# Batch 0 of a chunked attention with a sine network: values computed transposed, normalisers spread by TensorE, memory values loaded apart, and a new order of the opening

## The chip, the cores and the metric

The kernel runs on one core of a Trainium2 chip. The metric is the device time of one execution in microseconds (us); a kernel's time is the median of its runs. The engines are written as in the profile: PE (TensorE matmuls), PEld (its weight loads), DVE (VectorE), ACT (ScalarE), POOL (GpSimd), SP (SyncE). Each engine works through its own list of instructions in order and waits where data from another engine or from a DMA is not there yet.

## The reference

Two parts follow each other. First a chunked attention over 4 batches, 8 heads, 768 positions of 64 numbers each, in 24 chunks of 32 queries. A chunk sees 8 memory keys, and the positions from 16 ahead of it to 8 behind it:

```python
k_full = np.concatenate([mem_k, k_ctx], axis=2)
v_full = np.concatenate([mem_v, v_ctx], axis=2)
scores = scale * np.matmul(q_c, k_full.transpose(0, 1, 3, 2))
scores = scores - np.max(scores, axis=-1, keepdims=True)
a = np.exp(scores)
a = a / (np.sum(a, axis=-1, keepdims=True) + 1e-09)
out[:, :, c_start:c_end] = np.matmul(a, v_full)
```

Then a network with a sine in it, on the 3072 positions with their 8 heads side by side (512 numbers):

```python
h = x @ w_in                      # 512 x 2048
s = np.sin(alpha * h)
g = h + s * s / (alpha + 1e-09)
return (g @ w_out).astype(np.float32)   # 2048 x 512
```

Inputs and output are fp32; the kernel multiplies in bf16.

## The kernel before

**Stages.** Everything is unrolled. A batch is 768 positions, cut into 8 windows of 96 queries (QW, three chunks each), a half is 4 windows (HALF, 384 queries). The opening ("front", stage -1) does the attention of batch 0. Then stage i (0 to 3) does the network of batch i, with the attention of batch i + 1 woven in. In a stage, `half_tile` (L422) makes one half of a tile of 128 of the 2048 inner columns with 4 matmuls against w_in (L424), `sine`, `squared` and `finish` (L435 to L456) make g of it, and `second` (L458) multiplies with w_out (L462).

**Order.** The order is written out by hand: a string of words per stage, read by `Stage.run` (L525); the first letter picks the method, the rest are its arguments. This order is the order of the instructions on each engine; there is no other scheduler. The words of the front:

- `a` n engine: cast tile n of the fp32 loads (0 to 3 are k of head pairs 0 to 3, 4 to 7 q) to bf16, L653
- `k`, `l`: turn a head pair's k or q on PE (12 transposes, L274); `K`, `L`: copy it out of PSUM into kT or qT (L285, L291, L299)
- `s` hp half: masked scores of a head pair and a half on PE (L317, L325), then the exponential on ACT into a tile pt (L332)
- `v` hp half: values (L344), then normalising on DVE (L353, L354) into x_blk; `t`, `T`: turn x_blk on PE (L366) and copy it into xT on DVE or ACT (L369). xT is what the network of stage 0 reads
- `V` b h0 h1: load v of heads h0 to h1 with POOL's DMAs (L172, L179; L168 too for head 0); the windows overlap, so rows come twice, and the DMA casts to bf16
- `dm`: load all memory values with one POOL DMA (L665); `m` 0: spread those of batch 0 into rows 64 to 71 of vw on DVE (L188)
- `C` x: constants: `b`, `m`, `i` for the mask, `k` the memory keys (cast L767, turned L771, copied L775 and into kT L207), `l` alpha (turned L785, L786, L787), `p`, `z`, `v`, `s` memsets on POOL
- `I` a b: load columns of w_in by tiles on POOL's queue (L213); `U`: rows of w_out (L219)
- `z` n: n matmuls of zeros (L686); `We`, `Ws`: one small Exp or Sin on ACT (L699), by which the table of that function is loaded
- stage 0 goes on with `o8 b0 h0 ...`: `b` and `h` are the two halves of a tile of the network

**Queues.** SP's queue brings the eight fp32 loads of k and q of batch 0 (L708, 384 KB each), ACT's the memory keys (L716, twice) and alpha (L717), POOL's all that is cast on its way: v, the weights, later k and q. `Banks` (L59) hands out the 8 PSUM banks; a bank given back may be taken again at once, and the new user then waits on the chip for the old one's last reader. It prefers a bank whose neighbour is in use.

**Values before.** In `u_values` (L339) the exponentials are the stationary operand and V, with a column of ones, moves, so that the queries lie on the partitions of the result and its column 64 holds the sums:

```python
nc.tensor.matmul(
    otv[:, e, i, :], pt[:, HALF * e + QW * i:HALF * e + QW * i + P],
    vws[b % 2][:, 2 * hp + e, 4 * half + i, 0:D + 1],
)
```

`normed` (L350) divides by it and `u_turn` (L372) turns the block, because the network needs the 512 numbers on partitions.

## Time and profile before

| what | value |
|---|---|
| time, median of 3 runs | 215.51 us (215.49 to 216.0) |
| span of the profiled execution (first to last instruction) | 213.1 us |
| instructions | 4479 |
| busy: PE, PEld, DVE, ACT, POOL | 201.7, 113.5, 140.5, 143.5, 99.8 us |
| granted clock of TensorE | 1.000 |
| DMA | 28.19 MB, mean 132 GB/s |

The profiled execution has no time of its own beside its span; the 2.4 us between the span and the median lie around the instructions. All starts below are us from the first instruction. In a timeline row stand start, duration, engine, line, operation, what is written and read, the shape, how many instructions are merged into the row, and in brackets how long the engine was idle ahead of it and what released it. "DMA" rows of the chain run from a transfer's issue to its landing. A row of a DMA issue ends with the KB of one transfer and the median us from issue to landing.

### The profile page before, as it was taken

What the parts mean: (1) busy time and instruction counts of PE and PEld (TensorE: products, weight loads), DVE (VectorE), ACT (ScalarE), POOL (GpSimd) and SP (SyncE); (2) the same over time, 40 slices, a digit from 0 to 9 for tenths busy, and PEclk for the clock granted to TensorE, in tenths of its full rate; (3) what the DMA queues carried; (4) which work ended last, traced back from release to release, by engine and by line L of the source; (5) the groups of instructions that cost most, each with busy time, mean ns of one, the idle gap of its engine ahead of it and who ended that gap; (6) DMA issues with size and microseconds to landing.
All of it is one profiled execution on the core that took longest, in us unless ns stands there. A gap on an engine that the chain in (4) does not pass through costs nothing.

```text
span 213.1 us, 4479 instructions
## 1 busy us (share of the span) xinstructions
PE 201.7 (95%) x1721; PEld 113.5 (53%) x1721; DVE 140.5 (66%) x218; ACT 143.5 (67%) x230; POOL 99.8 (47%) x140
## 2 busy tenths in 40 slices
PE   0799899999999999999999999999999999999994
PEld 0456555565455556555455555554555555554443
DVE  7598678999542749975856649898157197865011
ACT  2597898976857469977846199887846289891110
POOL 8959515688598193009991039659400023200000
PEclk9999999999999999999999999999999999999999
DMA  6999999999999999969999229989945400000312
GB/s 195 337 163 141 193 209 205 204 163 182 131 177 141 137 148 144 180 88 110 126 217 171 72 63 131 156 126 129 175 115 123 124 15 0 2 3 0 148 49 98
DMA packets 95908, 28.19 MB, mean 132 GB/s; under 512 B 84864, under 2 KB 92432, under 8 KB 95888
## 3 DMA queue, kind: packets, MB, share of 16 engines
q0 software_dynamic: 68736, 13.25, 92.3%
q1 hardware_dynamic: 26976, 14.62, 28.2%
q8 instruction: 13, 0.21, 0.4%
q14 instruction: 7, 0.06, 0.1%
q10 hardware_dynamic: 176, 0.04, 0.1%
HBM read 29.66 MB, written 6.29 MB: 169 GB/s over the span
## 4 chain that ended last, share of the span: by engine, by line
PE 71%; DVE 9%; DMA 7%; ACT 4%; issue 4%; POOL 3%; DVEq 0%; POOLq 0%; ACTq 0%
PE ps L462 38%; PE ps L424 27%; DMA memv_st<-in_mem_v_dram 4%; DVE gT L451 4%; DVE s L447 3%; DMA vw<-in_v_dram 3%; PE ps L414 3%; PE ps L385 2%; ACT u L439 2%; PE ps L366 1%; ACT s L444 1%; POOL s L447 1%; POOL vw L172 1%; DVE kT L285 1%; ACT L699 1%
## 5 line engine op out<-in xcount | busy, mean ns | idle before, releaser
L462 PE MATMUL ps<-w_out_sb,gT 128*128 128x512 bf16 (+2 forms) x400 | 89.1, 371 | 0.0
L424 PE MATMUL ps<-xT,w_in_sb 128*128 128x384 bf16 x512 | 86.0, 326 | 0.7 <-DVE gT L451 0.4
L451 DVE SCALAR_TENSOR_TENSOR gT<-s,inv_alpha,ps 128x768 bf16<-128x768 f32 x64 | 63.0, 1011 | 12.5 <-ACT s L444 5.2
L424 PEld LDWEIGHTS <-w_in_sb 128*128 128x128 bf16 x512 | 49.8, 98 | 35.4 <-issue 2.1
L439 ACT ACTIVATE u<-ps,alpha_sb 128x768 f32<-128x768 f32 x64 | 56.6, 895 | 16.8 <-PE ps L424 14.3
L462 PEld LDWEIGHTS <-gT 128*128 128x128 bf16 x400 | 36.6, 98 | 37.9 <-DVE gT L451 0.2
L447 POOL TENSOR_TENSOR s<-u 128x768 f32<-128x768 f32 x11 | 17.4, 1582 | 69.7 <-ACT u L439 69.7
L399 ACT ACTIVATE pt<-ps,biasm 128x256 bf16<-128x256 f32 x72 | 27.2, 489 | 10.5 <-PE ps L385 10.5
L469 DVE COPY o_sb<-ps 128x512 f32<-128x512 f32 (+1 forms) x15 | 10.1, 678 | 28.3 <-PE ps L462 26.4
L447 DVE TENSOR_TENSOR s<-u 128x768 f32<-128x768 f32 x23 | 21.9, 953 | 7.8 <-ACT u L439 7.8
L444 ACT ACTIVATE s<-u 128x768 f32<-128x768 f32 x30 | 25.0, 841 | 0.5
L354 DVE TENSOR_TENSOR x_blk<-ps,rinv 96x512 bf16<-96x512 f32 x32 | 22.0, 687 | 1.1
L469 ACT COPY o_sb<-ps 128x512 f32<-128x512 f32 (+1 forms) x10 | 5.6, 562 | 21.6 <-PE ps L462 21.6
L172 POOL DMA_DIRECT2D vw<-in_v_dram x13 | 12.9, 994 | 7.9 <-PE ps L366 5.4
L353 DVE RECIPROCAL rinv<-ps 96x8 f32<-96x8 f32 x32 | 6.4, 200 | 13.5 <-PE ps L414 12.7
L179 POOL DMA_DIRECT2D vw<-in_v_dram x13 | 12.7, 976 | 0.0
L238 POOL DMA_DIRECT2D kst<-in_k_dram x16 | 12.2, 760 | 1.1 <-DMA vw<-in_v_dram 0.8
L232 POOL DMA_DIRECT2D kst<-in_k_dram x16 | 11.3, 708 | 2.3 <-DMA vw<-in_v_dram 1.6
L369 ACT COPY xT<-ps 128x384 bf16<-128x384 bf16 x12 | 5.6, 496 | 8.2 <-PE ps L366 8.2
L245 POOL DMA_DIRECT2D q_bf<-in_q_dram x12 | 10.7, 912 | 0.0
L414 PEld LDWEIGHTS <-pt 128*128 128x128 bf16 x192 | 8.2, 97 | 4.2 <-ACT pt L399 0.3
L414 PE MATMUL ps<-vw,pt 128*128 128x65 bf16 x192 | 8.9, 193 | 0.0
(81 smaller groups left out, 131.4 us busy)
## 6 DMA issues: line engine op xcount, KB each, us to landing
out_dram<-o_sb SPq DMA_DIRECT2D x23, 256.0 KB, 2.3
kq_f<-in_k_dram SPq DMA_DIRECT2D x4, 384.0 KB, 6.5
kq_f<-in_q_dram SPq DMA_DIRECT2D x4, 384.0 KB, 6.0
q_bf<-in_q_dram POOLq DMA_DIRECT2D x12, 128.0 KB, 6.7
w_in_sb<-in_moe_w_in_dram POOLq DMA_DIRECT2D x1, 1152.0 KB, 12.6
vw<-in_v_dram POOLq DMA_DIRECT2D x7, 128.0 KB, 6.7
vw<-in_v_dram POOLq DMA_DIRECT2D x8, 112.0 KB, 7.4
kst<-in_k_dram POOLq DMA_DIRECT2D x14, 64.0 KB, 5.1
```

What stands on the lines that cost most here:

```text
L172: nc.gpsimd.dma_start(vw[0:64, lo:c1, 0:D], win(vflat, a, n, 64))
L179: nc.gpsimd.dma_start(vw[72:128, c0:hi, 0:D], win(vflat, base + QW * c0 + 48, hi - c0, 56))
L354: nc.vector.tensor_tensor(out=x_blk[:].rearrange("p g e d -> p e g d"), in0=otv[0:QW, :, :, 0:D], in1=rinv[:].unsqueeze(3).to_broadcast([Q ...
L399: nc.scalar.activation(pt[:, 0:H * QW].rearrange("p (g e c) -> p g e c", g=2, e=4)[:, :, :, 32 * m:32 * m + 32], sc[:, :, 0:4 * QW].rearra ...
L414: nc.tensor.matmul(otv[:, e, hp, :], pt[:, QW * i:QW * i + P], vws[b % 2][:, 2 * hp + e, j, 0:D + 1],)
L424: nc.tensor.matmul(t["hT"][:, hf, 0:HALF], w_in_sb[:, kt, P * t["ft"]:P * t["ft"] + P], t["xT"][:, kt, HALF * hf:HALF * hf + HALF], start= ...
L439: nc.scalar.activation(t["u"][:], t["hT"][:, :, 0:HALF], ACTF.Sin, scale=alpha_sb[:, ft:ft + 1])
L444: nc.scalar.activation(s2[:], u[:], ACTF.Square)
L447: e.tensor_tensor(out=s2[:], in0=u[:], in1=u[:], op=ALU.mult)
L451: nc.vector.scalar_tensor_tensor(out=gT[:, ft, :].rearrange("p (e c) -> p e c", e=2), in0=t["s2"][:], scalar=inv_alpha[:, ft:ft + 1], in1= ...
L462: nc.tensor.matmul(o[:, c0:c1], gT[:, ft, P * s:P * s + P], w_out_sb[:, ft, c0:c1], start=(ft == 0), stop=(ft == FT - 1),)
L469: copier(state["engines"][state["o"] % len(state["engines"])])(o_sb[:, c0:c1], o[:, c0:c1])
```

## The change

For batch 0 alone:

- the values are computed with V stationary and the exponentials moving, so that the result has the head's 64 numbers on partitions, two heads in the upper and lower half, and goes to xT with one multiplication on DVE; the turning and its copies go away for batch 0
- the sums are made apart (word `n`, for a head pair: 16 matmuls with one column of ones, a reciprocal, and its split into two bf16 parts), and spread over 64 partitions by PE (word `r`: 32 matmuls with a broadcast column as the stationary operand and the identity moving), then copied to SBUF in fp32
- the memory values of batch 0 come in fp32 on ACT's queue and are cast on DVE (`Cw`); `dm` brings the other three batches
- the memory keys are turned in fp32, without the cast ahead of it; `ident_f` is larger, and made in a word of its own (`Cf`)
- the words of the front stand in a new order; those of the stages are the same (their lines are only broken elsewhere)

```diff
+    ones = consts.tile([P, 2], BF, name="ones")
-    memk_bf = memv_st[0:NK, 0]
-    ident_f = consts.tile([FT, FT], F32, name="ident_f")
+    ident_f = consts.tile([4 * FT, 4 * FT], F32, name="ident_f")
...
-    def u_values(b, hp, half, pt):
-        ot, bs = banks.pair()
-        otv = ot[:, :, 0:4 * (D + 1)].rearrange("p e (g c) -> p e g c", c=D + 1)
-        for e in range(2):
+    rs = {}
+
+    def u_sums(hp, two):
+        bank, bs = banks.single()
+        sums = bank[:, 0:2 * H]
+        for half in range(2):
+            for c in range(H):
+                nc.tensor.matmul(sums[:, H * half + c:H * half + c + 1],
+                                 two[half][:, QW * c:QW * c + P], ones[:, 0:1])
+        rinv = blk.tile([QW, 2 * H], F32, name="r_inv", bufs=2)
+        hi = blk.tile([QW, 2 * H], BF, name="r_hi", bufs=2)
+        lo = blk.tile([QW, 2 * H], BF, name="r_lo", bufs=2)
+        nc.vector.reciprocal(rinv[:], sums[0:QW])
+        nc.vector.tensor_copy(hi[:], rinv[:])
+        nc.vector.tensor_tensor(out=lo[:], in0=rinv[:], in1=hi[:], op=ALU.subtract)
+        banks.give(bs)
+        return hi, lo
+
+    def u_spread(hp, got, eng):
+        t, bs = banks.pair()
+        for half in range(2):
             for i in range(4):
+                for part in range(2):
+                    for e in range(2):
+                        c = H * half + 4 * e + i
+                        nc.tensor.matmul(
+                            t[64 * e:64 * e + 64, half, QW * i:QW * i + QW],
+                            got[part][:, c:c + 1].to_broadcast([QW, D]),
+                            ident[0:QW, 0:QW], start=(part == 0), stop=(part == 1),
+                        )
+        rs[hp] = mlp.tile([P, 2, HALF], F32, name="r_sb", tag="s2")
+        copier(eng)(rs[hp][:], t[:, :, 0:HALF])
+        banks.give(bs)
+
+    def u_values(xT, hp, half, pt):
+        bank, bs = banks.single()
+        for i in range(4):
+            for e in range(2):
                 nc.tensor.matmul(
-                    otv[:, e, i, :], pt[:, HALF * e + QW * i:HALF * e + QW * i + P],
-                    vws[b % 2][:, 2 * hp + e, 4 * half + i, 0:D + 1],
+                    bank[64 * e:64 * e + 64, QW * i:QW * i + QW],
+                    vws[0][:, 2 * hp + e, 4 * half + i, 0:D],
+                    pt[:, HALF * e + QW * i:HALF * e + QW * i + QW],
                 )
-        return normed(otv, bs)
+        nc.vector.tensor_tensor(
+            out=xT[:, hp, HALF * half:HALF * half + HALF],
+            in0=bank[:, 0:HALF], in1=rs[hp][:, half], op=ALU.mult,
+        )
+        banks.give(bs)
...
-                nc.gpsimd.dma_start(memv_st[64:72].rearrange("n b h d -> n (b h) d"),
-                                    mem_v.rearrange("b h n d -> n (b h) d"))
+                nc.gpsimd.dma_start(memv_st[64:72, 1:].rearrange("n b h d -> n (b h) d"),
+                                    mem_v[1:].rearrange("b h n d -> n (b h) d"))
...
+    memv_f = mlp.tile([P, H, D], F32, name="memv_f", tag="o_sb", bufs=3)
...
     nc.scalar.dma_start(alpha_rows[:], moe_alpha.rearrange("(ft p) -> ft p", p=P))
+    nc.scalar.dma_start(memv_f[64:72], mem_v[0].rearrange("h n d -> n h d"))
...
     def const_k():
-        nc.vector.tensor_copy(memk_bf, memk_f[0:NK])
         bank, bs = banks.single()
-        mt = bank[:, 0:2 * NK].bitcast(BF).rearrange("p (g c) -> p g c", g=HP)
+        mt = bank[:, 0:HP * NK].rearrange("p (g c) -> p g c", g=HP)
         for g in range(HP):
             nc.tensor.transpose(
-                mt[:, g, :], memk_bf[:, 2 * g:2 * g + 2, :].rearrange("p e d -> p (e d)"),
-                ident[0:NK, 0:NK]
+                mt[:, g, :], memk_f[0:NK, 2 * g:2 * g + 2, :].rearrange("p e d -> p (e d)"),
+                ident_f[0:NK, 0:NK]
             )
...
+    def const_f():
+        nc.vector.tensor_copy(ident_f[:], ident[0:4 * FT, 0:4 * FT])
+
+    def const_w():
+        nc.vector.tensor_copy(memv_st[64:72, 0], memv_f[64:72])
+
     def const_l():
-        nc.vector.tensor_copy(ident_f[:], ident[0:FT, 0:FT])
...
     stage.run((
-        'a1A Cb Cp Cz Cv a5A eVA Cm Cl z4 a0V Ci k0 dm a4V l0 k1 K0V Ck l1 L0A V024 We L1V a2A K1A V002 '
-        'a6V k2 s00 K2V a3V s11 V068 m0 a7V s01 l2 s10 k3 K3A L2A V046 z4 v10 l3 Cs L3A I02 v11 s20 z1 '
-        'v01 s30 z1 v00 s31 z1 v30 s21 v31 T01 T10 v20 T30 T00 v21 T20 T31 I27 t11 t21 eVA Ws '
+        'Cb Cv a0V a4A a1A a5A z4 Cf Cw dm m0 Cm z2 k0 We Ck k1 K0V V068 Cl Cz K1A a2A l1 Ci L1V '
+        'l0 k2 V024 Cp L0A K2V V002 a3V s10 eVA s11 s00 V046 a6V I02 a7V s01 n1 k3 l2 K3V L2A l3 '
+        'L3A n0 Cs s20 r1A r0V s30 v10 s21 v11 s31 n2 v00 n3 v01 r2A r3A v20 eVA v21 v30 z1 Ws '
+        'v31 I27 '
     ))
```

Of the new functions, `do_n` calls `u_sums` with both halves of a head pair, `do_r` calls `u_spread`, and `do_v` of batch 0 calls the new `u_values`.

More of the change, by code (lines that the diff above doesn't have):

```diff
@@ L370, in turned @@
         banks.give(bs)
-    def u_turn(xT, hp, half, x_blk, eng="V"):
-        turned(
-            x_blk,
-            xT[:, hp, HALF * half:HALF * half + HALF].rearrange("p (g c) -> p g c", g=4), eng)
     def scores(b, js):
@@ L508, in __init__ @@
             self.b = i + 1
-            self.tile, self.piece, self.pt, self.xb = {}, {}, {}, {}
+            self.tile, self.piece, self.pt, self.xb, self.rb = {}, {}, {}, {}, {}
             self.done = 0
@@ L611, in turn_x @@
             x_blk = self.xb.pop(a)
-            if self.b == 0:
-                u_turn(x, int(a[0]), int(a[1]), x_blk, eng)
-            else:
-                turned(x_blk, x[:, :, QW * int(a):QW * int(a) + QW], eng)
+            turned(x_blk, x[:, :, QW * int(a):QW * int(a) + QW], eng)
             xslots.give(x_blk)
@@ L624, in do_c @@
         def do_c(self, a):
[L625 to L630 removed]
+            c0 = QW * int(a)
+            x = self.next_x()[:, :, c0:c0 + QW]
             x_blk = self.xb.pop(a)
@@ L722 @@
     nc.vector.memset(tiny[:], 0.0)
+    nc.vector.memset(ones[:], 1.0)
     nc.vector.memset(mcol[:], 0.0)
@@ L807 @@
     consts_of = dict(b=const_b, m=const_m, i=const_i, k=const_k, l=const_l, p=const_p, v=const_v,
-                     s=const_s, z=const_z)
+                     s=const_s, z=const_z, f=const_f, w=const_w)
     first = {}
```

14 lines of the change are left out of this document (6 added, 8 removed), and 38 rows, old and new, of the table stage.

## The prediction

> **What bounds the kernel now.** I read first the page's span, then busy time by stretch, then the timeline of the first 25 us, then the chain of waits.
>
> ```profile
> span 213.1 us, 4479 instructions
> ```
> ```profile
> 20.00:25.00 5.00, 4.07 (x77) 3.07 (x77) 4.16 (x10) 4.05 (x8) 4.49 (x7) 1.00 1.29 182
> 25.00:30.00 5.00, 5.00 (x32) 3.01 (x31) 2.46 (x4) 4.66 (x7) 0.54 (x1) 1.00 1.11 211
> 80.00:100.00 20.00, 19.99 (x118) 11.35 (x117) 15.89 (x18) 17.64 (x25) 5.65 (x6) 1.00 1.36 131
> ```
> In the stretches the fields after the length are PE, PEld, DVE, ACT and POOL busy. From 25 us on PE is filled (5.00 of 5, later 19.99 of 20); ahead of that it is not.
>
> ```profile
> 24.81 17.62 PE L424 MATMUL ps<-xT,w_in_sb 128*128 128x384 bf16 x104
> 25.05 1.28 ACT L699 ACT_TABLE_LOAD   x1
> ```
> The first product with w_in starts at 24.81, and 104 of them take 17.62, or 0.169 each, without a hole. So all after 24.81 is a PE list that moves as a block: a front later by x makes the kernel later by x. The change lies wholly in the front (its word list, and the functions of batch 0), so I forecast one number: when tile 0 of stage 0 is through both halves. Now that is 24.81 + 8 x 0.169 = 26.16.
>
> What ends the front? The chain of waits:
>
> ```profile
> 4.86 9.20 DMA memv_st<-in_mem_v_dram
> 14.34 1.75 POOL vw L172
> 16.09 6.06 DMA vw<-in_v_dram
> 22.29 0.43 PE ps L344 x8
> ```
> Memory values on POOL's queue land after 9.2 us, at 14.06; the ninth of POOL's DMAs had waited for it; its pair lands at 16.09 + 6.06 = 22.15; then come values, normalising, turning, copying, and the start at 24.8. By this the chain is a chain of DMAs. But it holds PE up for only 0.25 us:
>
> ```profile
> 22.29 0.42 PE L344 MATMUL ps<-vw,pt 128*128 128x65 bf16 x8 [0.25 <-DMA vw<-in_v_dram]
> ```
> So a second limit stands right behind the DMA: the list of each engine, in order. I worked that out too, by laying the words of the front in order on PE, DVE and ACT with the durations quoted below, 0.05 us a hop between engines, and banks freed in the order of Banks. For the kernel before, this gives 26.13 for the end of tile 0, against 26.16 in the trace. I use the same sums for the change.
>
> **The change part by part.** *Memory values.* They leave POOL's queue for ScalarE's, as the fourth small transfer there, right behind alpha. They land in fp32, so VectorE casts them (Cw), spreads them (m0), and only then reaches everything after them, because these words stand near the head of its list. When do they land? The nearest row:
>
> ```profile
> 1.69 0.42 ACTq L717 DMA_DIRECT2D alpha_rows<-in_moe_alpha_dram  x1
> alpha_rows<-in_moe_alpha_dram ACTq DMA_DIRECT2D x1, 8.0 KB, 4.3
> kq_f<-in_q_dram SPq DMA_DIRECT2D x4, 384.0 KB, 6.0
> ```
> Issued behind alpha at about 2.11, with alpha's 4.3 us it lands at 6.4; with the 6.0 of a large load issued beside it, at 8.1. I take 6.5, since it is small like alpha's. What VectorE then does:
>
> ```profile
> 10.06 0.40 DVE L767 CAST memv_st<-memk_f 16x512 bf16<-16x512 f32 x1
> 14.45 1.22 DVE L188 COPY vw<-memv_st 8x4096 bf16<-8x4096 bf16 x1
> 4.90 0.23 DVE L754 COPY mrow<-ps 128x128 bf16<-128x128 bf16 x1 [0.38 <-PE ps L753]
> 10.81 0.19 DVE L775 COPY memkT<-ps 128x64 bf16<-128x64 bf16 x1 [0.35 <-PE ps L771]
> 11.04 0.36 DVE L207 COPY kT<-memkT 128x256 bf16<-128x256 bf16 x2
> 8.99 0.86 DVE L285 COPY kT<-ps 128x672 bf16<-128x672 bf16 x1 [0.95 <-PE ps L274]
> 9.89 0.26 DVE L291 COPY kT<-ps 128x96 bf16<-128x96 bf16 x1
> 6.39 0.17 DVE L786 COPY alpha_sb<-ps 128x16 f32<-128x16 f32 x1 [1.19 <-PE ps L785]
> 6.60 0.25 DVE L787 RECIPROCAL inv_alpha<-alpha_sb 128x16 f32<-128x16 f32 x1
> 11.32 0.95 DVE L299 COPY qT<-ps 128x768 bf16<-128x768 bf16 x1
> ```
> Cw 0.40 (taken from the cast of memory keys, L767), m0 1.22, mask 0.23, memory keys 0.19 + 0.36, K0V 0.86 + 0.26, alpha 0.17 + 0.25, K1's ends 0.26, L1V 0.95: 5.14 us. There is one wait inside: alpha's transposition takes the bank of k0, which K0V frees, so VectorE waits some 0.45 for PE. With the hops L1V ends at 6.5 + 5.14 + 0.45 + 0.15 = 12.25. What waits behind it: k1 on PE takes the bank of the memory keys, whose copy is VectorE's fifth word after the landing (8.5), and every PE word after k1 stands behind that. The first scores (s10) need L1V.
>
> *Scores.* The four exponentials before L2A stand back to back on ScalarE, and then L2A:
>
> ```profile
> 12.31 3.04 ACT L332 ACTIVATE pt<-ps 128x768 bf16<-128x768 f32 x4 [0.45 <-PE ps L325]
> 17.89 0.81 ACT L332 ACTIVATE pt<-ps 128x768 bf16<-128x768 f32 x1
> 9.63 0.80 ACT L299 COPY qT<-ps 128x768 bf16<-128x768 bf16 x1 [0.44 <-PE ps L274]
> ```
> From 12.25: s10 on PE 0.55, four exponentials of 0.81 3.25, L2A 0.80, hops 0.2: 17.05, and s20 starts at 17.1. In the kernel before, s20's mask stands at 17.34 (below), so up to here nothing is won or lost. The earlier release that the words aim at is used up by the cast and the spread at the head of VectorE's list.
>
> *From s20 on* PE has the long list. Its group costs, from start to next start:
>
> ```profile
> 16.98 0.43 PE L344 MATMUL ps<-vw,pt 128*128 128x65 bf16 x8
> 17.34 0.34 PE L317 MATMUL ps<-mind,mrow 64*128 64x384 bf16 x2
> 17.51 0.33 PE L325 MATMUL ps<-qT,kT 64*128 64x96 bf16 x8
> 17.77 0.39 PE L686 MATMUL ps<-zeros 128*128 128x512 bf16 x1
> 18.08 0.42 PE L344 MATMUL ps<-vw,pt 128*128 128x65 bf16 x8
> 14.47 0.53 PE L274 MATMUL ps<-ident,k_bf 128*64 128x128 bf16 x12
> ```
> Values 17.34 - 16.98 = 0.36; scores 17.77 - 17.34 = 0.43; zeros 0.30. Within a group of values a matmul takes (0.43 - 0.19)/7, some 0.033, with 128 x 128 weights of its own. So one *n* (16 matmuls of one column, each with such weights) is 16 x 0.033 and a gap of 0.08: 0.60. The bounds: 0.43 if the gap is hidden and 0.027 holds for one column, 1.1 if each costs twice as much. One *r* is 32 matmuls of 96 columns on half the array's columns: L274's 12 are such, of 128 columns, at (0.53 - 0.22)/11 = 0.028, so 96 columns make 0.021: 32 x 0.021 + 0.1 = 0.77. Bounds 0.67 and, with weights not hidden, 1.44. *v* falls from 0.36 to 4 pairs x 0.043 + 0.1 = 0.27.
>
> [...]
>
> The list from s20 to the first word of stage 0: scores s20, s30, s21, s31 4 x 0.44 = 1.76; four r 3.08; n2 and n3 1.20; eight v 2.16; z1 0.30; n2 waits 0.35 for the exponential of s21 and z1 0.15 for a bank; 9.0. It starts at 17.1 and ends at 26.1-26.3. Before, the same stretch went from 17.34 to 24.81, 7.5, with eight turns and their waits for the copies in it.
>
> What lies beside: the copies of r. One copies 128 x 768 fp32 from PSUM, so I take for ScalarE 0.90 from L439 and for VectorE 0.95 from L299; each product on VectorE is 128 x 384, from L354's 512 columns 0.15 + 384 x 0.00104 = 0.55; an n on VectorE 0.2 for the reciprocal and 0.3 for two small ones.
>
> ```profile
> L439 ACT ACTIVATE u<-ps,alpha_sb 128x768 f32<-128x768 f32 x64 | 56.6, 895 | 16.8 <-PE ps L424 14.3
> L354 DVE TENSOR_TENSOR x_blk<-ps,rinv 96x512 bf16<-96x512 f32 x32 | 22.0, 687 | 1.1
> L353 DVE RECIPROCAL rinv<-ps 96x8 f32<-96x8 f32 x32 | 6.4, 200 | 13.5 <-PE ps L414 12.7
> ```
> ScalarE: exponentials end at 22.2, r2A and r3A follow PE's r2 and r3 to 25.9, the table of Sin (1.28 above, and 0.2) to 27.4: hidden, since the first Sin needs tile 0. VectorE: the products of v30 and v31 end at 26.9 and 27.5; tile 0's fourth matmul waits 0.13 for the first of them. The end of tile 0: 26.2 + 1.35 + 0.1 = 27.65, that is **1.5 later**.
>
> *Two surcharges.* dm and V068 are issued some 2 us earlier, and sooner take a part of the transfers that bring k and q; 1 us on those makes 0.15. And PE idles:
>
> ```profile
> 8.10 0.85 PE L274 MATMUL ps<-ident,k_bf 128*64 128x128 bf16 x12
> kq_f<-in_k_dram SPq DMA_DIRECT2D x1, 384.0 KB, 3.9
> ```
> At 8.10 a turn took 0.85, later 0.53: PE starts at half its pace. In the new order it turns k0 at 5.3 (the first load, issued at 0.76, lands after 3.9; then a cast of 0.55) and then waits for VectorE until 8.7. If the slow pace lasts up to 12 us, that makes 0.35-0.5; if not, nothing; I take 0.25. [...]
>
> *At nothing:* the fp32 turn of memory keys (in PE's wait until 8.7), const_f, the batch split of dm, the order of v (the last lands at about 22.2, PE comes to v20 at 24.7: 2.5 us of cover; were it gone, v's landing would end the front, as now). w_in of tiles 2 to 6 now lands 0.8 ahead of its use (the second of three issues, 18.03 + 0.76 + 7.9 = 26.7, used at 24.81 + 16 x 0.169 = 27.5); a later front only widens that.
>
> ```profile
> 18.03 2.27 POOL L213 DMA_DIRECT2D w_in_sb<-in_moe_w_in_dram  x3
> w_in_sb<-in_moe_w_in_dram POOLq DMA_DIRECT2D x1, 640.0 KB, 7.9
> ```
>
> **Sum.** Front +1.5 + 0.15 + 0.25 = +1.9. The profiled execution: span 213.1 + 1.9 = 215.0; 2.4 lie around it (215.51, the median, less 213.1), which I leave as they are: **217.4**.
>
> **The rivals.** (a) *The DMA chain is all there is, and the kernel gets faster.* For it: the chain of waits names nothing else after 4.86. Then PE stands at v20 when the last v lands (22.15), four groups of v and four products of 0.55 follow, and tile 0 ends at about 25.0: 1.1 earlier; w_in's 0.8 of slack (above) then binds. Time 215.5 - 0.8 = 214.7. It decides if PE gets from s20 to v20 in 5.0 us instead of 7.6. Against: even with n and r at zero my sum gives 26.2, because four exponentials, L2A, four more and two copies of r leave ScalarE no earlier end. Chance 0.12: the sums leave out what I can't see.
> (b) *It comes out even.* memv_f lands by 5.5 (VectorE then waits for k0's turn instead) and n, r cost 0.5 and 0.7: 26.5, +0.3, 215.8. Chance 0.20.
> (c) *The new load does not do what it says:* it queues with the large loads and lands at 8.1. VectorE's head and all after it shift one for one: +1.6 more, 219.0. Chance 0.11.
> (d) *The broadcast weights of r are not hidden* (nearest row L274, whose weights lie side by side): r 1.44, 4 x 0.67 = 2.7 more, 220.1. Chance 0.10. [...]
>
> **How the numbers follow.** Forecast 0.47, its own range 216.4 to 218.6 (n from 0.5 to 0.8, landing from 6.0 to 7.2). What tells a change from none is about 0.3%, 0.65 us: 214.9 to 216.2. Faster 0.12 (a), same 0.20 (b), slower 0.68 (forecast, c, d). Range 215.3 to 219.6: it leaves out (a) and about 0.07 of (b) and (d) together.
>
> **What would show it.** memv_f landing at 6 to 7; VectorE waiting at Cw for it (1 to 2 us) and PE ahead of k1 for 2 us or more; s20 at about 17; n near 0.6 and r near 0.77; PE without waits from there to the first L424 at about 26.3; no wait of PE for vw. Wrong if: PE waits for vw at v20 (then a), or the first L424 stands ahead of 25.

## The result and the profile after

The changed kernel takes 224.26 us (median of four runs, 223.03 to 225.45), the kernel before in the same session 215.50. The ratio is 1.039, with a 95% interval of 1.034 to 1.043: 8.8 us slower, where 1.9 were forecast and 219.6 was the upper end of the range. Some executions of one and the same kernel come out more than 1.5% above its fastest; the medians in this document include them, the ratios do not. The execution that was profiled took 225.45 us and is the longest of the four, so what is explained below is its 10.3 us of span and not the 8.8 us of the median.

From its page the span, and from the view of busy time by stretch the first 20 us after the scores (fields after the length: PE, PEld, DVE, ACT, POOL busy, granted clock of PE, DMA share, GB/s):

```profile
span 223.4 us, 4778 instructions
```
```profile
20.00:25.00 5.00, 4.80 (x154) 4.01 (x149) 3.32 (x9) 3.73 (x5) 4.57 (x7) 1.00 1.12 175
25.00:30.00 5.00, 2.31 (x64) 2.17 (x60) 1.31 (x5) 0.65 (x1) 0.53 (x1) 0.73 1.11 212
30.00:35.00 5.00, 4.53 (x59) 3.15 (x56) 2.04 (x4) 2.66 (x5) 0.00 (x0) 0.59 1.25 203
35.00:40.00 5.00, 5.00 (x33) 3.00 (x31) 3.99 (x5) 4.50 (x6) 0.00 (x0) 1.00 1.32 205
```

Before, PE was filled from 25 us on (5.00 of 5). Now it stands still for more than half of the stretch from 25 to 30, and from there to 35 its clock is granted at 0.59. Only from 35 on does it look as it did.

The start of the chain of waits (start, length, what) has a new first link. Memory values no longer hold up POOL; they hold up DVE:

```profile
2.15 5.95 DMA memv_f<-in_mem_v_dram
8.12 0.82 DVE memv_st L819
8.96 1.29 DVE vw L188
10.29 0.23 DVE mrow L789
```

They land at 8.10, not at 6.5; the cast takes 0.82, not 0.40. What stands behind it on the list of PE, from the timeline (start, length, engine, line, operation, operands; in brackets the idle time before it and what ended it):

```profile
10.70 0.85 PE L274 MATMUL ps<-ident,k_bf 128*64 128x128 bf16 x12 [4.63 <-DVE memkT L809]
14.43 0.50 PE L317 MATMUL ps<-mind,mrow 64*128 64x384 bf16 x2
19.19 0.34 PE L317 MATMUL ps<-mind,mrow 64*128 64x384 bf16 x2
...
19.71 0.23 PE L364 MATMUL ps<-ident,r_hi 96*64 96x96 bf16 x2
19.75 0.23 PE L364 MATMUL ps<-ident,r_lo 96*64 96x96 bf16 x2
...
24.30 0.55 PE L346 MATMUL ps<-ones,pt 128*128 128x1 bf16 x16
24.78 0.36 PE L377 MATMUL ps<-pt,vw 128*64 128x96 bf16 x8
24.98 0.21 PE L364 MATMUL ps<-ident,r_hi 96*64 96x96 bf16 x1
27.88 0.24 PE L364 MATMUL ps<-ident,r_hi 96*64 96x96 bf16 x1 [2.69 <-issue]
27.88 0.32 PE L364 MATMUL ps<-ident,r_lo 96*64 96x96 bf16 x2
...
30.29 0.31 PE L364 MATMUL ps<-ident,r_lo 96*64 96x96 bf16 x2
32.49 3.71 PE L457 MATMUL ps<-xT,w_in_sb 128*128 128x384 bf16 x17
```

Read it from the top. The turn k1 waited 4.63 us for memkT, which stands behind the landing on DVE's list. The scores s10 start at 14.43, s20 at 19.19 (forecast 17.1). Then r2 issues one matmul at 24.98, and the next one at 27.88. The 2.69 of idle time between them have "issue" as their cause: no semaphore, no DMA of data. Behind it a pair of r's matmuls takes 0.080 (27.88 to 30.29, 30 pairs), where a pair of r1 took 0.042 (19.71 to 19.75 and on). The first product with w_in (L457 now) starts at 32.49 instead of 24.81.

How long does the shift stay? I compared the start of each `u` activation, one per tile, in the two traces. The first is 8.32 later (26.45 and 34.77), and all through stages 0 to 2 the shift is 8.24. In stage 3 it is 9.91. The span differs by 10.3. So there are two places to explain: the front, and something between stages 2 and 3.

One more reading of the trace led to the theory. The page has a DMA queue of the kind "instruction", q8, and counts 13 of its packets before and 14 after; in the trace each is of 16384 bytes:

```profile
q8 instruction: 13, 0.21, 0.4%
```
```profile
q8 instruction: 14, 0.23, 0.5%
```

In the trace of after, one such packet (a fetch, from here on) starts at 25.46 and ends at 26.40, in the middle of the stop; PE goes on 1.48 later. The packet ahead of it ends at 19.31, and PE resumes 1.47 later, at 20.78, after a stop of 0.4 between r1 and r0. (The profile puts the last 0.2 of that one down to an exponential on ScalarE that ends at 20.69, so by itself it could be either.) Counted as rows of the trace (each matmul, each weight load and each of PE's few other instructions is one), these are PE's 450th and 706th rows: 256 apart. In all PE has 3468 rows before and 3761 after, 13.5 and 14.7 times 256, beside 13 and 14 packets; so I take q8's packets for PE's instructions.

**Theory.** The loss in the front is three costs in a row. (1) memv_f lands late, at DVE's head. (2) PE gets its instructions in blocks of 256 rows; the list with n and r uses up a block in 4.2 us (20.78 to 24.98), and the next one comes 7.1 us after the last (20.78 to 27.88), so PE runs dry. (3) Behind that PE runs at half its clock (granted 0.50 from 27.26 to 34.09). Ahead of stage 3 a fetch (171.33 to 173.16) slows the issue of one of SP's transposing DMAs (2.90 us, where most take 1.2). **Rivals.** The stop belongs to r itself (its broadcast weights, or r_lo); or it is a consequence of the late landing; or the new order of the words makes the loss.

### The profile page after: what moved, and what is told of

The parts are those of the page before. It is cut to its first block, busy times and chain, and to the rows that moved or that the text cites. A ratio compares the mean times of both kernels' runs of the same rounds, so it can differ in the third digit from the quotient of the medians.

```text
span 223.4 us, 4778 instructions
## 1 busy us (share of the span) xinstructions
PE 206.3 (92%) x1858; PEld 119.4 (53%) x1877; DVE 140.6 (63%) x222; ACT 143.3 (64%) x227; POOL 100.5 (45%) x140
## 4 chain that ended last, share of the span: by engine, by line
PE 77%; DVE 8%; issue 5%; DMA 4%; ACT 3%; SPq 1%; POOL 1%; ACTq 1%; DVEq 0%
PE ps L495 33%; PE ps L457 31%; DMA memv_f<-in_mem_v_dram 3%; PE ps L447 2%; DVE gT L484 2%; PE ps L418 2%; PE ps L364 2%; DVE s L480 2%; PE ps L274 1%; SPq L665 1%; ACT u L472 1%; PE ps L377 1%; PE ps L317 1%; ACT s L477 1%; DVE kT L285 1%
## 5 line engine op out<-in xcount | busy, mean ns | idle before, releaser
L457 PE MATMUL ps<-xT,w_in_sb 128*128 128x384 bf16 x512 | 86.9, 328 | 2.0 <-DMA xT<-x_blk 1.5
L495 PE MATMUL ps<-w_out_sb,gT 128*128 128x512 bf16 (+2 forms) x382 | 86.9, 370 | 1.3 <-issue 0.3
L457 PEld LDWEIGHTS <-w_in_sb 128*128 128x128 bf16 x512 | 49.9, 98 | 37.5 <-issue 4.6
L392 DVE TENSOR_TENSOR x_blk<-ps,rinv 96x512 bf16<-96x512 f32 x24 | 16.5, 687 | 0.8
L172 POOL DMA_DIRECT2D vw<-in_v_dram x13 | 11.8, 912 | 5.9 <-PE ps L404 5.9
L179 POOL DMA_DIRECT2D vw<-in_v_dram x13 | 12.9, 996 | 2.4 <-DMA vw<-in_v_dram 2.4
L238 POOL DMA_DIRECT2D kst<-in_k_dram x16 | 12.7, 793 | 0.8 <-DMA vw<-in_v_dram 0.8
L391 DVE RECIPROCAL rinv<-ps 96x8 f32<-96x8 f32 x24 | 4.8, 199 | 12.7 <-PE ps L447 12.7
L232 POOL DMA_DIRECT2D kst<-in_k_dram x16 | 11.8, 736 | 1.2 <-DMA vw<-in_v_dram 1.2
L274 PE MATMUL ps<-ident,k_bf 128*64 128x128 bf16 x96 | 5.0, 255 | 5.0 <-DVE memkT L809 4.6
```

The costliest lines, as they stand in the source:

```text
L179: nc.gpsimd.dma_start(vw[72:128, c0:hi, 0:D], win(vflat, base + QW * c0 + 48, hi - c0, 56))
L238: nc.gpsimd.dma_start(kst[72:72 + n, j, :].rearrange("p (h d) -> p h d", d=D), k[b, :, QW * j + 48:QW * j + 48 + n, :].rearrange("h p d -> ...
L392: nc.vector.tensor_tensor(out=x_blk[:].rearrange("p g e d -> p e g d"), in0=otv[0:QW, :, :, 0:D], in1=rinv[:].unsqueeze(3).to_broadcast([Q ...
L457: nc.tensor.matmul(t["hT"][:, hf, 0:HALF], w_in_sb[:, kt, P * t["ft"]:P * t["ft"] + P], t["xT"][:, kt, HALF * hf:HALF * hf + HALF], start= ...
L495: nc.tensor.matmul(o[:, c0:c1], gT[:, ft, P * s:P * s + P], w_out_sb[:, ft, c0:c1], start=(ft == 0), stop=(ft == FT - 1),)
```

## The experiments

Each ratio is to the kernel before, run on the same chip beside it.

### Does the stop follow the program or the count of rows? (pad64, r_hi)

pad64 adds 64 matmuls on zeros in PE's idle time, 128 rows; `y n` is a new word that makes n of them:

```diff
-k0 We Ck k1
+k0 We y32 Ck y32 k1
+    nc.tensor.matmul(ps[:, b, 0:1], zeros[:, 0:P], zeros[:, 0:1])
```

> The changed kernel with 64 matmuls of one column on zeros put into TensorE's idle time around the turn of the memory keys (32 ahead of it, 32 behind), 128 rows more in TensorE's list, no work for any result. Theory (the stop at 24.98 is the end of a block of 256 instructions): the stop moves 128 rows up in the program, to the scores s31 (after L317 or L325, near 23), and is again 2 to 3.5 us long with no r near it; the next block then ends inside r3, where a second stop can stand; time 224 to 228. Rival (r2 itself stops, by its broadcast weights or by a result that it reads): the stop stays at the second matmul of r2; time 224 to 225, or later by what the 64 matmuls don't find idle.

r_hi leaves the low part of the normalisers out of r:

```diff
-for part in range(2):
-    ... got[part][:, c:c + 1] ..., start=(part == 0), stop=(part == 1)
+    ... got[0][:, c:c + 1] ...
```

> The changed kernel with the low part of the normalisers left out of r: 16 matmuls instead of 32 in each of the four r, so the low half of each normaliser's bits is missing. TensorE has 1.4 us less to do. Theory (blocks of 256 instructions): the stop moves from r2 to the first matmuls of v20, just behind r3, because 64 rows fewer stand ahead of it, and it is as long as before, ending near 27.9; the time falls by 0.5 to 1.2 to 223.0 to 223.8. Rival (r and its weights are what stops TensorE): the stop shrinks to half or goes, time 220 or less.

PE's timeline, first pad64, then r_hi:

```profile
20.93 0.28 PE L377 MATMUL ps<-pt,vw 128*64 128x96 bf16 x4 [0.49 <-issue]
26.89 0.70 PE L377 MATMUL ps<-pt,vw 128*64 128x96 bf16 x23 [2.08 <-issue]
```
```profile
21.60 0.34 PE L317 MATMUL ps<-mind,mrow 64*128 64x384 bf16 x2 [0.79 <-issue]
...
26.10 0.21 PE L376 MATMUL ps<-pt,vw 128*64 128x96 bf16 x1
28.39 1.17 PE L376 MATMUL ps<-pt,vw 128*64 128x96 bf16 x23 [2.08 <-issue]
```

In pad64 nothing stops inside r2. PE stops in the middle of v11 and behind the first matmul of v20: again rows 706 and 962. The first of the two is 0.49 long, far shorter than the 2 to 3.5 that I expected. In r_hi it stops ahead of the scores s30 (0.79, row 450) and behind the first matmul of v20 (2.08), where row 706 now lies, and r2 and r3 run through. So the count of rows decides, and r is not what stops. Times: pad64 221.37 (ratio 1.026, 1.021 to 1.030), below the 224 to 228 that I expected; r_hi 220.77 (1.020, 1.015 to 1.024), below 223. I had taken the landing of memory values as fixed. It is not: in pad64 it came early, and the scores s20 stand at 17.03 and not at 19.19. In r_hi it came at 8.7; there the halved r may pay, and a shorter stretch at half the clock (3.4 us from 27.95 on, against 6.8 from 27.26 on in the changed kernel); the two are not told apart.

```profile
6.73 0.42 DVE L824 CAST memv_st<-memv_f 8x512 bf16<-8x512 f32 x1 [1.35 <-DMA memv_f<-in_mem_v_dram]
17.03 0.34 PE L317 MATMUL ps<-mind,mrow 64*128 64x384 bf16 x2
```

### What the late landing costs (late_spread, mem_first)

late_spread takes the cast and the spread away from DVE's head; mem_first issues the load first:

```diff
 late_spread
-z4 Cf Cw dm m0 Cm z2 ...  K2V V002 a3V
+z4 Cf dm Cm z2 ...  K2V Cw m0 V002 a3V
 mem_first
+nc.scalar.dma_start(memv_f[64:72], mem_v[0].rearrange("h n d -> n h d"))
 for bb in range(B): ... dma_start(memk_f[...
 nc.scalar.dma_start(alpha_rows[:], ...
-nc.scalar.dma_start(memv_f[64:72], mem_v[0].rearrange("h n d -> n h d"))
```

> The changed kernel with the cast and the spread of the memory values (Cw, m0) moved behind K2V, so that nothing ahead of K2V on VectorE waits for their transfer. Theory (three costs in a row: late landing at the head of VectorE, then TensorE without instructions, then half the clock): the scores s10 start some 2 us earlier than 14.43, so near 12.4, but TensorE still comes to its 706th row, the second matmul of r2, within about 4.2 us of its 450th and finds no instructions there, so a stop of 2 to 4 us stays at r2; time 221 to 223. Rival (the late landing is all there is, and the stop at r2 is its consequence): no stop at r2, the clock stays whole, time near 217.

> The changed kernel with the load of memory values issued first on ScalarE's queue, ahead of the memory keys and alpha, so some 1 us earlier. Theory (landing at VectorE's head is the first of three costs): it lands at 5 to 7 instead of 8.10; s10 starts at 12.4 to 13.0 instead of 14.43; TensorE still stops at its 706th row for 1 to 3 us (some 1.5 us earlier by the clock of the span), and half the clock follows; time 221 to 223. Rival (all follows from the landing): with the landing no later than the 6.5 of the forecast, no stop and time 217 to 218.5. Rival (the landing doesn't matter): time 224 or more.

late_spread: 221.16 (1.022, 1.018 to 1.026), inside the range, and by another way than I thought. s10 does start 2 us earlier (12.47), but the 1.6 us of cast and spread now stand ahead of the casts of k and q, PE waits for those, and s20 is no earlier than in the changed kernel. PE's timeline, and the stretch behind it:

```profile
16.32 0.53 PE L274 MATMUL ps<-ident,k_bf 128*64 128x128 bf16 x12 [0.84 <-DVE k_bf L685]
17.12 0.53 PE L274 MATMUL ps<-ident,q_bf 128*64 128x128 bf16 x12 [0.28 <-DVE q_bf L685]
18.00 0.85 PE L274 MATMUL ps<-ident,q_bf 128*64 128x128 bf16 x12 [0.35 <-DVE q_bf L685]
19.30 0.50 PE L317 MATMUL ps<-mind,mrow 64*128 64x384 bf16 x2
```
```profile
18.00:25.00 7.00, 7.00 (x138) 5.64 (x138) 3.62 (x10) 3.88 (x6) 6.03 (x9) 0.51 1.65 181
```

From 18.0 to 24.9 the clock is granted at half (0.51 in the stretch), behind three waits for casts (0.84, 0.28 and 0.35). At half the pace PE comes to row 706 only at 27.0, and no stop stands there. So my expectation of a stop was wrong, and the theory needs its third part to be read with the second: here the half clock, which came first, hides the stop.

mem_first is the cleaner test. DVE's timeline and PE's:

```profile
5.25 0.63 DVE L819 CAST memv_st<-memv_f 8x512 bf16<-8x512 f32 x1
16.84 0.34 PE L317 MATMUL ps<-mind,mrow 64*128 64x384 bf16 x2
...
23.32 0.21 PE L364 MATMUL ps<-ident,r_hi 96*64 96x96 bf16 x1
25.12 0.20 PE L364 MATMUL ps<-ident,r_hi 96*64 96x96 bf16 x1 [1.59 <-issue]
27.85 2.40 PE L457 MATMUL ps<-xT,w_in_sb 128*128 128x384 bf16 x13
```

Landed by 5.2, cast and spread lie in DVE's wait for the first turn of k. s20 stands at 16.84: the 17.1 of the forecast holds once the landing is no later than forecast. The stop at row 706 is there all the same, 1.8 us (23.32 to 25.12), so it is no consequence of the landing. There is also a wait of 1.1 at row 450 (17.98 to 19.12), where the copy of r1 ends too, so that I can't divide it. The clock stays whole in this execution, which I had not expected. Three of its executions show what the clock goes with: 219.03 with a mean granted clock of 1.000, 220.14 and 220.87 with 0.992, so 1.1 to 1.8 us for 0.008 (a mean 0.008 lower over 218 us is 3.5 us at half the clock). 220.50 (1.020, 1.013 to 1.026), just under my 221 to 223.

### Clock and instructions together (warm)

```diff
-k0 We Ck k1 ... s01 n1 k3 l2 K3V L2A l3
+k0 z6 We Ck z2 k1 ... s01 n1 z4 k3 z2 l2 K3V L2A z2 l3
```

on top of late_spread: matmuls on zeros in PE's waits.

> late_spread with 16 matmuls on zeros of 512 columns in TensorE's waits: 6 behind k0, 2 behind the memory keys, 4 ahead of k3, 2 each ahead of l2 and l3 (32 rows more). Theory (the half pace of late_spread from 18 to 24.7 comes from TensorE's waits before it; and with the whole pace TensorE outruns its instructions): a pair of matmuls of r takes 0.042 instead of 0.080 between 18 and 25, TensorE comes to its 706th row more than 1 us earlier than in late_spread, and there it stops, 1 to 3 us; the time changes little, 219 to 222. Rival A (the clock is not a matter of the waits): r stays at 0.080, time as late_spread, 221 plus what of the zeros isn't hidden. Rival B (no limit on instructions here): r at 0.042, no stop, 217 to 218.

```profile
24.13 0.38 PE L346 MATMUL ps<-ones,pt 128*128 128x1 bf16 x9
26.33 0.31 PE L346 MATMUL ps<-ones,pt 128*128 128x1 bf16 x7 [1.82 <-issue]
```

As the theory has it: the clock is whole from 10 to 27 (granted 1.00), a pair of r takes 0.042, PE comes to row 706 at 24.35 (in late_spread 27.0) and then stops for 1.82 in the middle of n3. A part of the 2.6 us is that the zeros are 32 rows themselves, so that row 706 lies 32 rows earlier in the program. Behind the stop the clock falls after all, to half from 27.1 to 30.5 (granted 0.50). 220.13 (1.020, 1.011 to 1.028), against 1.022 for late_spread: what the clock gave ahead of the stop, the stop and the half clock behind it took.

### How fast instructions come, and what lets the clock fall (burst, burst_r)

Both are the kernel before with a run of matmuls on zeros put in; 300 of one column at two places (burst), or 300 in the form of r's at the second place alone (burst_r):

```diff
-V158 b11 ... q14A q13V g14 g13
+V158 y300 b11 ... q14A q13V g14 g13 y300      (burst)
+V158 b11 ... q14A q13V g14 g13 y300           (burst_r)
+    nc.tensor.matmul(ps[0:D, b, 0:QW], zeros[0:QW, 0:D], zeros[0:QW, 0:QW])   (burst_r)
```

> The kernel before with 300 matmuls of one column on zeros (600 rows) put in twice: behind V158 in stage 0, where transfers run all the time (near 40 us), and behind the last g of the last stage, where next to none run (near 195 us). It measures how fast TensorE is given instructions. Theory (blocks of 256 rows; a refill takes 6 to 7 us among transfers): in stage 0 the 256 rows of a block take 3.5 to 4.5 us and a stop of 2 to 3.5 us follows each; in the last stage a refill is 4 us or less and the stops are under 1 us; 20 to 30 us longer in all, 236 to 246. Rival (the refill takes 6 to 7 us wherever it is): the same stops of 2 to 3.5 us at both places. Rival (no limit by blocks): both bursts run through in about 10 us without a stop over 0.3.

> The kernel before with 300 matmuls in the form of those of r (96 columns on zeros, weights of 96 x 64, one half of the array's columns) behind the last g of the last stage, where next to no transfers run. It tells which matmuls let the clock fall: 300 of one column at the same place did so after 5.8 us without any idle time. Theory (the throttle weighs how much of the time columns move, not how many matmuls there are): 0.042 each, 12.6 us in all, whole clock throughout and behind it, no stop; time 226 to 229. Rival (short matmuls with their own weights let the clock fall whatever their columns): half the clock from some 6 us on, 0.080 each, 18 to 22 us in all; time 233 to 238.

PE's timeline in burst, and two stretches of its busy time:

```profile
39.51 5.94 PE L691 MATMUL ps<-zeros 128*128 128x1 bf16 x228
47.41 2.08 PE L691 MATMUL ps<-zeros 128*128 128x1 bf16 x72 [1.97 <-issue]
202.03 7.78 PE L691 MATMUL ps<-zeros 128*128 128x1 bf16 x300
```
```profile
39.50:45.40 5.90, 5.90 (x230) 5.85 (x227) 3.31 (x4) 1.81 (x3) 1.01 (x1) 0.86 1.31 204
203.00:212.00 9.00, 9.00 (x273) 7.53 (x271) 3.73 (x4) 1.78 (x3) 0.00 (x0) 0.76 0.02 4
```

In stage 0, with 204 GB/s of transfers, PE stops for 1.97 after 228 of the 300, at row 1218, which is 450 + 3 x 256. So one stop came there, where I had expected one behind each block. In the last stage, with 4 GB/s, the 600 rows run through at 0.025 a matmul: a block of 256 rows lasts 3.2 us there, and the next one is in, though only just (its packet ends at 206.19, and its first row starts 1.4 later). The trace shows which part of a fetch differs: the packet itself takes 0.9 to 1.4 at both places, but it starts 2.8 us after PE enters a block in stage 0 (row 962, 128 matmuls ahead of the stop at 45.28, so at 42.0; packet at 44.81), 4.7 in the front of the changed kernel (20.78 to 25.46), and some 0.4 and 1.1 in the last stage. How much data moves does not settle it: by the same count of rows the fetch just before, in the same trace, starts 1.5 us after row 706 (34.46 to 35.98) with 203 GB/s, and in the kernel before the one behind row 962 after 1.3 (49.81 to 51.07) with 201. What holds a fetch back for 2.8 to 4.7 us stays open. 237.18, in the range.

The clock fell in both bursts, and not because PE stood idle: in the last stage there is no gap, and the clock is at half (granted 0.50) from 207.6 on, 5.6 us after the first of them; in stage 0 it is at half from 43.8 on, 4.2 us after the first and ahead of the stop. burst_r has the same number of matmuls at that place:

```profile
194.82 12.83 PE L691 MATMUL ps<-zeros 96*64 96x96 bf16 x298
```
```profile
200.00:208.00 8.00, 8.00 (x183) 7.73 (x180) 0.00 (x0) 0.00 (x0) 0.00 (x0) 1.00 0.02 4
208.00:212.00 4.00, 4.00 (x20) 1.85 (x19) 0.00 (x0) 0.00 (x0) 0.00 (x0) 1.00 0.00 0
```

With 96 columns each the clock stays at 1.00, and a matmul takes 0.043 (12.83 / 298). So it isn't the number of matmuls that counts. That it is how much of the time columns move is a guess of mine from these two, 1 column in 0.025 us and 96 in 0.043, and not shown: their weights (128 x 128 and 96 x 64) and their pace differ too. The two runs of burst_r took 229.2 and 233.1, both above the 226 to 229 expected; the longer one was profiled, and its excess lies outside the burst.

In the changed kernel the clock changes at 17.02, 27.26 and 34.09, so 10.24 and 6.83 apart, which is three times and twice 3.41, the step used below; in warm it is at half for one such step (27.1 to 30.5).

### What is left without n and r (no_norm, order_old, order_old_late, before_load)

no_norm leaves the normalisation of batch 0 out (n and r go, the product is with 0.01), and its cast and spread stand behind a7V. order_old keeps the new load and order, but computes the values as before:

```diff
 no_norm
-... s01 n1 k3 l2 K3V L2A l3 L3A n0 Cs s20 r1A r0V s30 v10 s21 v11 s31 n2 v00 n3 v01 r2A r3A v20 ...
+... Cw m0 s01 k3 l2 K3V L2A l3 L3A Cs s20 s30 v10 s21 v11 s31 v00 v01 v20 ...
 order_old
+... s01 k3 l2 K3V L2A l3 L3A z4 v10 Cs v11 s20 z1 v01 s30 z1 v00 s31 z1 v30 s21 v31 T01 T10 v20 T30 ...
 order_old_late: order_old with
-Cf Cw dm m0 Cm ... a7V s01
+Cf dm Cm ... a7V Cw m0 s01
 before_load: the kernel before with memv_f on ScalarE's queue and
-V068 m0 a7V
+V068 Cw m0 a7V
```

> The changed kernel without its normalisers: the words n and r are left out, and each product with a normaliser is a product with the constant 0.01, so batch 0's attention isn't normalised; the cast and the spread of memory values stand behind a7V. 384 rows fewer on TensorE. Theory (the new way of computing values is cheap; its price are the 192 matmuls of n and r, their blocks of instructions and the clock behind them): no stop at a block's end over 0.4 us, whole clock from 18 on, the first L457 at 23.3 to 24.2, where the transfers of w_in then bind; span 211.7 to 212.8, time 214.0 to 215.2. Rival (the earlier transfers of V, or the late landing, cost whatever is computed): first L457 at 26 or later, time 217 or more.

> The changed kernel with the old way of computing the values of batch 0 (queries moving through V with a column of ones, normalised on VectorE, turned by TensorE): the new load, the new head of the list and the cast at VectorE's head are kept, n and r go, and from v10 on the words are those of the kernel before. Theory (landing at VectorE's head, then blocks and clock through n and r): only the first cost is left; s20 at 18 to 19.5, no stop at a block's end over 0.5, clock whole from 18 on, first L457 at 26.3 to 27.8, time 217.0 to 218.6. Rival (the new order and load make the whole loss): first L457 beyond 29, time 221 or more.

> order_old (the old way of computing values in the new order) with the cast and the spread of memory values behind a7V, so that VectorE's head waits for no transfer. Theory (what order_old still loses, 1.6 us of the span, is the landing at VectorE's head): s10 at 12.4 to 13, first L424 at 24.5 to 25.4 instead of 26.60, time 215.0 to 216.2, level with the kernel before. Rival (the order of the other words loses it): first L424 at 26 or later, time 216.5 or more.

> The kernel before with one part of the change alone: memory values of batch 0 in fp32 by ScalarE's queue, cast behind V068 just ahead of m0; values, normalisers and the order of all else as before. The DMAs of V then start some 2 us earlier on POOL's queue. Theory (the landing costs only where it stands at VectorE's head, and the list of each engine ends the front, not V's DMAs): within 0.5 us of the kernel before, 215.0 to 216.0. Rival (V's DMAs end the front): the wait of TensorE for vw at 22.29 goes and 0.5 to 1.1 us are won, 214.4 to 215.0. Rival (the earlier transfers collide with those of k and q): 0.7 us or more lost, above 216.2.

The start of the first product with w_in, from the timelines of no_norm, order_old and order_old_late, one fence each:

```profile
23.42 3.33 PE L455 MATMUL ps<-xT,w_in_sb 128*128 128x384 bf16 x18
```
```profile
26.60 1.63 PE L428 MATMUL ps<-xT,w_in_sb 128*128 128x384 bf16 x9
```
```profile
18.39 0.68 PE L346 MATMUL ps<-vw,pt 128*128 128x65 bf16 x16 [0.75 <-DVE vw L188]
26.76 0.49 PE L428 MATMUL ps<-xT,w_in_sb 128*128 128x384 bf16 x2
```

no_norm: 214.18 (0.993, 0.987 to 1.000), as expected, though the interval just reaches the kernel before, and with no stop over 0.4 at a block's end. The new way of computing values is cheap: the first product stands 1.4 us earlier than before; but this is with normalisers at no cost, so it is a bound: its tiles are 0.95 earlier from stage 1 on, and n and r would have to cost less than that to win. (The clock did fall, to 0.50 from 20 to 23, behind waits; that part of the expectation failed.)

order_old: 216.73 (1.004, 0.999 to 1.010), 0.3 under the range. Its memory values land at 8.1 as in the changed kernel, and of the 8.24 in stage 1, 1.57 are left. So the new way of computing values as a whole, n and r with what hangs on them less what it saves, makes 6.7 of the 8.24; landing, load and order make the rest.

In order_old_late I expected that rest to go with the landing. It did not: 217.45 (1.009, 1.006 to 1.013), first L428 at 26.76. Both are what the rival had said, that the order of the other words loses it. In the trace, cast and spread, moved behind a7V, hold up K3V and v10 (0.75 for vw in the row above). So my theory's first part was too narrow: 1.6 us of cast and spread are new or earlier work on DVE ahead of s20, and they seem to be free only where DVE waits anyway, as in mem_first. No run tells this apart from the order of the other words.

before_load: 218.13 (1.006, 1.003 to 1.010), so the expectation of "level" missed by 0.6%, and the time lies in the range of the second rival, that the earlier transfers collide with those of k and q. Its profile (an execution of 216.52) doesn't show that collision: the loads of k and q land a median of 5.6 us after their issue, 6.3 in the kernel before. The last pair of v lands at 21.71 instead of 22.15, and PE waits for vw only 0.09 in one place, yet the first product stands at 24.94, 0.13 later than before; the tiles are 0.3 late, and the end of the span is another 1.4 later. So V's DMAs were not what ended the front. Where the 0.6% goes stays open.

### The 1.67 us ahead of stage 3 (before_y24)

The change adds 312 rows to PE's list: 128 matmuls of r and 64 of n more, 32 of turning and 4 on zeros fewer, each with its weight load. That is 56 more than a block (the 305 and 49 of the expectation below were counted wrong), so from the front on all later blocks begin 56 rows earlier in the program. before_y24 gives the kernel before nearly the same offset, 8 rows short of it, with 48 rows in PE's first idle time:

```diff
-'a1A Cb Cp
+'y24 a1A Cb Cp
```

> The kernel before with 24 matmuls of one column on zeros at the very head of TensorE's list, in its first idle time: 48 rows more, as the change makes 305 = 256 + 49 more, so every later block of instructions begins at the same place of the program as in the changed kernel. Theory (the last 1.67 us of the loss come between stages 2 and 3, because TensorE's fetch of instructions falls into SP's issue of a transposing DMA and stretches it): stages 0 to 2 within 0.5 us of the kernel before; a fetch near 163 of the span, the issue of the transposition at 162.0 takes 2 us or more instead of 1.21, and from stage 3 on all is 0.5 to 1.7 us later; time 216.0 to 217.5. Rival (the 1.67 come from something else that the change brings, or from chance): the issue stays at 1.2 to 1.3, nothing is later, time 215.3 to 215.8.

SP's timeline of the four last transposing DMAs of stage 2 (L633 and L665 are the same line), in before, after and before_y24, and the wait that follows in after (waited for: in total, times, longest):

```profile
162.02 5.39 SPq L633 DMA_TRANSPOSE xT<-x_blk  x4
```
```profile
170.66 6.80 SPq L665 DMA_TRANSPOSE xT<-x_blk  x4
```
```profile
PE ps L457 <- DMA xT<-x_blk: 1.5, 1, 1.5
```
```profile
163.05 6.17 SPq L633 DMA_TRANSPOSE xT<-x_blk  x4
```

Four issues take 5.39 in before, 6.80 in after, 6.17 in before_y24. One by one, an issue takes 1.2; in after the first of the four takes 2.90, with a packet of PE's instructions from 171.33 to 173.16 inside it; in before_y24 the second takes 2.27, with a packet from 164.40 to 165.56. Over before, after, pad64, r_hi, late_spread and before_load the traces have 84 issues of that line: every one over 1.4 us has such a packet in it or under way as it starts. Not every packet does it; one that starts with the end of an issue leaves it at 1.2. From stage 3 on before_y24 is 0.76 later than in stage 2, the changed kernel 1.67, late_spread 0.55, pad64 0.61, mem_first 0.77, r_hi nothing (its packet lies before the last four). 216.18 (1.002, 0.999 to 1.006): in the range, but before_y24 had lost 0.9 in the front already, more than the 0.5 that I allowed (PE waited 1.13 for kT at 16.82 and 0.59 for vw at 19.41), so that its time alone proves little. The evidence is the issue and the step of 0.76; it is a coincidence seen in every slow issue, and how a fetch can slow one is not shown.

## Why the prediction was wrong

**What held.** The front shifts all behind it as a block: the shift is 8.24 through three stages. The schedule up to s20 held: 17.1 for a landing at 6.5, 17.03 and 16.84 measured for landings at 6.7 and 5.2. n and r were priced well: n 0.48 (24.30 to 24.78) for 0.60, r 0.74 (two from 17.51 to 18.99 in pad64) for 0.77, v 0.29 (24.01 to 24.30) for 0.27. Rival (d), weights not hidden, is out. PE never waited for vw, the copies of r were hidden, and rival (a), an end set by V's DMAs, is out by before_load. The sign was right. Two smaller slips: the lower bound of n took 0.027 for a matmul of one column, and quotes no row for it (four of 16 columns in the kernel before, L771, make (0.25 - 0.17)/3 = 0.027; burst measured 0.025 for one column); and the range left out more than the 0.07 of (b) and (d) that its text gives, since (d), with 0.10, stood at 220.1, above 219.6.

**The step that failed** is the one that begins "From s20 on PE has the long list": 9.0 us, added up from durations alone. It took 13.3 (19.19 to 32.49). In mem_first, where the clock stays whole, the same list took 11.0 (16.84 to 27.85); less the waits at rows 450 and 706 that is 8.1. The sum of durations was even too long; what it left out are the stops at rows 450 and 706 (0.4 and 2.9) and the half clock from 27.26 to 34.09. r's matmuls were taken at 0.021 each, 48 instructions of 96 columns in a microsecond with their weight loads as many again, and I never asked whether a row can be had that often. So the prediction's own sign for this stretch, PE without waits up to the first product, failed, and none of its rivals had a stop of this kind.

**The other terms.** memv_f's landing was sized at 6.5 from alpha's row and measured 8.10: rival (c), given 0.11. It also varies (6.7 to 8.7 in one execution each of four kernels with the same issue time). The surcharge of 0.25 for a slow PE was put ahead of s10, where the pace was indeed half (0.85 a turn at 10.70, 0.53 at 17.58); it stayed so up to 17.0 (0.50 for the mask of s10 at 14.43, 0.34 for that of s20), longer than the 12 us that the prediction allowed, but the dear stretch came behind the stop. And "all after 24.81 moves as a block" left out that the new rows shift every later fetch (the twelfth starts at 170.66 before and at 162.49 after).

The account of the profiled execution, in us, up to the first tile's `u`:

| term | us |
|---|---|
| forecast of the front, without surcharges | +1.5 |
| landing 8.10 for 6.5, cast 0.81 for 0.40 (s20 at 19.19 for 17.1) | +2.1 |
| list shorter than its sum (9.0 to the 8.1 of mem_first) | -0.9 |
| stops at rows 450 and 706 (0.4 and 2.9) | +3.3 |
| half clock: 27.88 to 32.49 is 4.6, in mem_first 2.7; then 5 products at 0.32 | +2.7 |
| sum; measured 8.3 | 8.7 |
| ahead of stage 3, transposition and fetch | +1.7 |
| end of the span another 0.4 later, not explained | +0.4 |

The parts of the front are not additive in general: late_spread and warm show that the half clock hides a stop. **Open:** whether the clock in the changed kernel fell for the stop of 2.9 or for the one-column matmuls of n2 and n3 ahead of it. In mem_first a stop of 1.8 behind the same n2 and n3 left it whole; in warm one of 2.0 did not. Where the stop falls against the steps of 3.41 us may decide, which is a guess of mine: in the step ahead of the fall PE stood idle for 2.1 us in the changed kernel, 2.3 in pad64, 1.9 in r_hi and 1.8 in warm, while mem_first's stop lies across the end of a step (23.58, three steps from 13.34) and leaves 1.5 in the next. But in late_spread the clock fell at 18.03 behind a step with 1.5 of idle time, so idle time alone is not it.

None of the versions that normalise beats the kernel before. The bound that no_norm sets, 0.993 with no normalisers at all, leaves this way of computing values about 1 us to give, and n and r take 4.9 us of PE's time (4 x 0.48 + 4 x 0.74).

## What to carry to other kernels

Where TensorE's list is made of short matmuls, count its rows (matmuls and weight loads) as well as its microseconds: at the longer stops here 256 rows took 5.3 to 7.1 us to come, and the changed kernel's list, which used them up in 4.2, stopped at the 256th row for 2.9; in pad64, r_hi and warm other matmuls stood there, and PE stopped for 2.0 to 2.3. A stop that the profile puts down to "issue" and that stays at the same row when the program is shifted is most likely this one. Before work is put at an engine's head behind a transfer, look for a place where that engine waits anyway; and where a change alters the number of instructions, look at the later fetches too: a loss far from the edit, as the 1.67 us ahead of stage 3 here, can still be its doing.

## What the runs showed of the hardware that I had not expected

- PE's stops stand 256 rows apart: at rows 450, 706 and 962 in five kernels with different programs, and at 1218 in burst. PE goes on 1.3 to 1.7 us after the end of a q8 packet (1.47 and 1.48 in after, 1.36 in r_hi, 1.33 in mem_first, 1.71 in burst).
- Ahead of the longer stops a fetch starts 2.8 to 4.7 us after a block is entered, with some 180 to 200 GB/s moving; with as much moving it also started after 1.3 and 1.5 us, and with 4 GB/s after 0.4 and 1.1.
- 300 one-column matmuls back to back run at 0.025 each and let the clock fall to half (0.50) 4.2 and 5.6 us after the first, without any gap; with 300 of 96 columns, 0.043 each, it stayed at 1.00.
- The issue of a transposing DMA on SP takes 1.2 us, and 1.5 to 2.9 in 13 of 84 cases, each with a packet of PE's instructions in it or under way as it starts; not every packet does it.
- A 16 KB load on ScalarE's queue, issued fourth beside large loads, took 6.0 us to land (2.15 to 8.10); issued first, it was there by 5.2.
